# Which partitions 80 rows of each wq-gradient group are sent from, and how the last gradients are stored, in a decode backward kernel

## The chip, the core and the metric

The kernel runs on one core of a Trainium2 chip. The metric is the device time of one execution in microseconds (us), the median of several runs: 729.89 us before the change (three runs, 729.66 to 730.07). Lower is better.

## The reference, cut to what matters

One token of width D = 640 goes through a layer norm, attention of 32 heads over a cache of 8192 positions, and beside it a gated MLP of width 1728. The kernel returns the output row and all gradients for a given `grad_out`.

```
xn  = layernorm(x)
q   = (xn @ wq) in 32 heads of 128;  p = softmax(q k^T / sqrt(128));  o = p v
out = x + o @ wo + (silu(xn @ w1) * (xn @ w3)) @ w2
gradients of sum(out * grad_out): x, k_cache, v_cache, wq, wo, w1, w3, w2
```

The caches are 32 x 8192 x 128 in bf16 each, so each head's K and V are 2 MB, read once, and their gradients are 2 MB each, written once. The gradient of `wq` (640 x 4096) is the outer product of xn and dq, and that of `wo` (4096 x 640) the outer product of o and `grad_out`.

## The kernel before, in words

**Heads.** The loop over h = 0 to 31 calls `head(h)`. A head's K and V lie in two of ten 2 MB buffers `kv0` to `kv9`. TensorE transposes them (L362), ScalarE copies the transposes out of PSUM (L364), TensorE forms scores and dP (L383), VectorE does the softmax's small steps (L426 to L494), TensorE sums (L477), and VectorE writes the K and V gradients over the K and V that they came from (`outer`, L510, four pieces of 128 x 4096 a head). `store` sends such a buffer to DRAM, and `load_next` then queues the next head's load into a free buffer. Loads and stores of K and V are issued by SyncE's queue (SP, `fifo` L106 and `fifo_wide` L111) in program order, so a load that waits for its buffer holds up the store behind it.

**MLP.** Before head 2 comes `mlp()`, whose weights lie in four of the ten buffers; it is followed by its weight gradients, which GpSimd (POOL) issues.

**Groups.** Heads come in eight groups of four. A group has a `wq_g` tile (128 partitions x 5 x 512: row ci * 128 + p of `wq` lies in partition p) and a `wo_g` tile. While the next group's heads run, the group's gradients are made (`fin_od`, `fin_pe`, `fin_wo`, `fin_wq`, spread over the heads by `side_k`, `side_m` and `side_v`), and GpSimd issues their stores. `fin_wq(g, ci)` makes 128 rows of 1 KB and sends them with an indirect DMA (`scatter`, L330): `row_idx` gives each partition its row in DRAM, and a row whose index is out of bounds is left out.

**Rows that leave from elsewhere.** `rel_setup`, called once ahead of the head loop, makes two sets of indices. It pushes out of bounds the indices of partitions 16 to 19 and 48 to 51 in the first four of the five ci. Those 32 rows of a group are made a second time in the tile `rel`, whose partitions 0 to 15 and 32 to 47 hold them (each partition scales the same row `dqb` by its own xn value, `rel_x`), and one more scatter with `rel_idx` sends them at the end of the group. All other indices of `rel_idx` are out of bounds.

**The last group.** Group 7 has no scatter. `store_group` (L549 to L555) sends its `wo_g` and `wq_g` in three transfers each: partitions 0 to 67 on SP's queue, 68 to 72 and 73 to 127 on GpSimd's.

**Order.** The order on each engine is the program's; nothing is rescheduled. In the prologue VectorE, TensorE and GpSimd do `rel_setup` between `rows_act(0)` and `head(0)`:

```
    rows_act(0)
    rel_setup()
    for h in range(H):
        if h == MLP_AT:
        ...
        head(h)
        if h < 2:
            nc.gpsimd.tensor_copy(gate[:], hd[h]["rdot"][:])
            load_group(h + 1, nc.gpsimd)
```

In `head(1)` the first steps are `outers_a(0)` (VectorE: both pieces of dV and one of dK of head 0, then dV's store) and the rest of head 1's K transposes (TensorE). `mx` (L426) is the first VectorE step that the scores of the head need, `col`, `fin_od` and others belong to later heads.

Of the kernel before, what the change touches and what calls it, by code (L numbers as in the profile page):

```python
# [21 lines left out]
def kernel(  # L22
# [22 lines left out]
    nc = tc.nc  # L45
# [14 lines left out]
    consts = ctx.enter_context(tc.tile_pool(name="consts", bufs=1))  # L60
# [20 lines left out]
    dwq_v = out_4.rearrange("(ci p) n -> p ci n", p=P)  # L81
    dwo_v = out_5.rearrange("(h p) c -> p h c", p=P)
# [22 lines left out]
    def fifo(out_, in_):  # L105
        nc.sync.dma_start(out_, in_)  # L106
# [10 lines left out]
    def load_group(g, eng):  # L117
        wq_g = wpool.tile([P, NC, GW], BF16, name="wq_g", tag="wq_g")
        eng.dma_start(wq_g[:], wq_v[:, :, g * GW:(g + 1) * GW])
        wo_g = wpool.tile([P, GH, D], BF16, name="wo_g", tag="wo_g")  # L120
        eng.dma_start(wo_g[:], wo_v[:, g * GH:(g + 1) * GH, :])
        grp[g] = dict(wq=wq_g, wo=wo_g)
# [47 lines left out]
    ident_f = consts.tile([P, P], F32, name="ident_f")  # L170
# [4 lines left out]
    pm_one = masks[:, 0:2]  # L175
# [45 lines left out]
    def pst():  # L221
        return ps_t.tile([P, 512], F32, name="pT", tag="pT")
# [5 lines left out]
    for ci in range(NC):  # L228
        nc.tensor.matmul(ps_xg[:, ci:ci + 1], lhsT=x_row[:, ci * P:(ci + 1) * P], rhs=one_bf[0:1, :],
                         start=True, stop=True)  # L230
        nc.tensor.matmul(ps_xg[:, NC + ci:NC + ci + 1], lhsT=g_row[:, ci * P:(ci + 1) * P], rhs=one_bf[0:1, :],
                         start=True, stop=True)
    nc.tensor.matmul(ps_xg[:, P:P + D - 512], lhsT=one_bf[0:1, :].to_broadcast([1, P]), rhs=g_row[:, 512:D],
                     start=True, stop=True)
    nc.tensor.matmul(ps_g[:], lhsT=one_bf[0:1, :].to_broadcast([1, P]), rhs=g_row[:, 0:512],
                     start=True, stop=True)
# [59 lines left out]
    NF4 = 4  # L296
    dwq_row = out_4.rearrange("d (k n) -> (d k) n", n=GW)
    row_idx = consts.tile([P, NC], I32, name="row_idx")
    rel_idx = consts.tile([P, 1], I32, name="rel_idx")
    rel_x = consts.tile([P, 1], F32, name="rel_x")  # L300
    rel = consts.tile([P, GW], BF16, name="rel")
    NREL = 48

    def rel_setup():
        nc.gpsimd.memset(rel[:], 0.0)
        w = kt_tile()[:].rearrange("p k w -> p (k w)")
        iv, off, far = w[:, 0:NC], w[:, 8:9], w[:, 16:17]
        nc.gpsimd.iota(row_idx[:], pattern=[[NG * P, NC]], base=0, channel_multiplier=NG)
        nc.vector.tensor_copy(iv, row_idx[:])
        ps_r = pst()  # L310
        for k, src in enumerate((xn_col[:], iv)):
            sx = w[:, 128 * (k + 1):128 * (k + 1) + NREL]
            nc.vector.memset(sx, 0.0)
            for b0 in (0, 32):
                nc.vector.tensor_tensor(
                    sx[:, b0:b0 + 4 * NF4].rearrange("p (c b) -> p c b", b=4),
                    src[:, 0:NF4].unsqueeze(2).to_broadcast([P, NF4, 4]),
                    ident_f[:, 16 + b0:20 + b0].unsqueeze(1).to_broadcast([P, NF4, 4]), ALU.mult)
            nc.tensor.matmul(ps_r[0:NREL, k:k + 1], lhsT=sx, rhs=pm_one[:, 0:1], start=True, stop=True)
        nc.vector.tensor_copy(rel_x[0:NREL], ps_r[0:NREL, 0:1])  # L320
        nc.vector.memset(far, 1048576.0)
        for b0 in (0, 32):
            nc.vector.tensor_copy(far[b0:b0 + 4 * NF4], ps_r[b0:b0 + 4 * NF4, 1:2])
        nc.vector.tensor_copy(rel_idx[:], far)
        nc.vector.tensor_reduce(off, ident_f[:, 16:80].rearrange("p (s r) -> p s r", r=32)[:, :, 0:4], AX.XY, ALU.add)
        nc.vector.tensor_scalar(off, off, 1048576.0, None, ALU.mult)
        nc.vector.tensor_scalar(row_idx[:, 0:NF4], iv[:, 0:NF4], off, None, ALU.add)
# [90 lines left out]
    def rows_act(h):  # L418
        qd = small.tile([P, 2, DH], BF16, name="qd")
        nc.scalar.copy(qd[:].rearrange("p a d -> p (a d)"), hd[h].pop("ps_r"))  # L420
        hd[h]["qd"] = qd
# [124 lines left out]
        for hh in range(GH):  # L546
            out_row(G_["od_bf"][:, hh, 0:1], G_["wo"][:, hh, :])

    def store_group(g, dst, t):  # L549
        if g < NG - 1:  # L550
            nc.gpsimd.dma_start(dst, t[:])  # L551
            return
        fifo(dst[0:68], t[0:68])
        for lo, hi in ((68, 73), (73, P)):
            nc.gpsimd.dma_start(dst[lo:hi], t[lo:hi])  # L555

    def fin_wo(g):
        G_ = grp[g]
        for hh in range(GH):
            nc.vector.tensor_scalar(G_["wo"][:, hh, :], g_bc[:], G_["od"][:, hh, 0:1], None, ALU.mult)  # L560
        store_group(g, dwo_v[:, g * GH:(g + 1) * GH, :], G_["wo"])

    def fin_wq(g, ci):
        G_ = grp[g]
        wq_g, dqb = G_["wq"], G_["dqb"]
        nc.vector.scalar_tensor_tensor(wq_g[:, ci, :], wq_g[:, ci, :], 1.0, dqb, ALU.mult, ALU.mult,  # L566
                                       accum_out=dxa[:, ci, g:g + 1])
        nc.vector.tensor_scalar(wq_g[:, ci, :], dqb, xn_col[:, ci:ci + 1], None, ALU.mult)
        dwq_g = dwq_v[:, :, g * GW:(g + 1) * GW]
# [222 lines left out]
    def head(h):  # L792
        nxt = h + 1 < H
        pre = nxt and h + 1 != MLP_AT
        has_prev = h > 0 and h != MLP_AT
        had = (4 if h else 2) if h != MLP_AT else 0
        if nxt:
            new_head(h + 1)
        if has_prev:
            outers_a(h - 1)  # L800
        side_k(h)
        for c in range(had, NCH, 2):
            T(h, "K", c)
# [12 lines left out]
        mx(h)  # L816
        Mp(h, "V", 0)
        T(h, "V", 4)
        mx_bc(h)
        side_m(h)  # L820
        T(h, "V", 5)
        Mp(h, "V", 2)
        expo(h)
        T(h, "V", 6)
        zsum(h)
        probs(h)
        if has_prev:
            outers_b(h - 1)
        side_pe1(h)
        T(h, "V", 7)  # L830
        side_pe1b(h)
        Mp(h, "V", 4)
        side_pe2(h)
        side_v(h)
        if nxt:
            fill_qz(h + 1)
            rows_pe(h + 1, pst()[:, 0:2 * DH], True)
            rows_act(h + 1)
        if pre:
            T(h + 1, "K", 0)  # L840
            T(h + 1, "K", 1)
        Mp(h, "V", NCH - 2)
        ev(h, "V")
        o_sum(h)
        selm(h, "V")
        rdot(h)
        if pre:
            T(h + 1, "K", 2)
        dsum(h)
        if pre:  # L850
            T(h + 1, "K", 3)
            Mp(h + 1, "K", 0)
        dq_sum(h)
        if not nxt:
            col(h)
# [90 lines left out]
```

## Time and profile before

| what | value |
|---|---|
| median of three runs | 729.89 us |
| the profiled execution, its own time | 733.47 us |
| its span, first to last instruction | 731.7 us |
| bytes moved, mean rate | 303.53 MB, 415 GB/s |
| TensorE matmul busy | 603.5 us, 82% |
| VectorE busy | 462.5 us, 63% |
| ScalarE busy | 376.9 us, 52% |
| GpSimd busy | 83.7 us, 11% |
| scatters of `wq_g` / of `rel` | 35 / 7, median 8.7 / 7.9 us from issue to landing |

The page's part 2 cuts the span into 40 slices of 18.3 us and gives each engine's busy share in tenths, then the share of time in which the 16 DMA engines had a packet, and the rate. Part 4 follows the work that ended last back to the start. The windows view sums the same for stretches that are asked for; there a DMA packet is counted in the stretch in which it starts. Beside these the trace holds each DMA packet (start, duration, size, queue, without the number of its engine) and each rise of a semaphore; a transfer over all 16 DMA engines raises its semaphore 16 times, once for each engine.

### The profile page before, as it was taken

How to read it: one execution, taken by the hardware profiler on the slowest of the kernel's cores; microseconds unless marked ns; L12 is line 12 of the kernel's file. 1: busy time of each engine (PE TensorE's matmuls, PEld its weight loads, DVE VectorE, ACT ScalarE, POOL GpSimd, SP SyncE). 2: the span in 40 equal slices, each digit the busy share in tenths (PEclk: the TensorE clock that was granted, in tenths of full speed). 3: DMA queues.
4: the chain of work that ended last, by engine and by line, in shares of the span. 5: the costliest groups of instructions: out<-in, count | busy, mean ns of one | idle time of the engine just before them, and what ended most of it. 6: DMA issues, size and time to landing. Idle time of an engine off the chain costs nothing.

```text
span 731.7 us, 13091 instructions
## 1 busy us (share of the span) xinstructions
PE 603.5 (82%) x5213; PEld 377.1 (52%) x5213; DVE 462.5 (63%) x829; ACT 376.9 (52%) x727; POOL 83.7 (11%) x84
## 2 busy tenths in 40 slices
PE   3989579999999999978896999788979889888820
PEld 2556456665566556545554556355545555555510
DVE  4168665777867886857645775656665676646780
ACT  3650726666666656645554556355655455545500
POOL 0010010002220011101110111011200110011110
PEclk9995799999999999999998999999999899989955
DMA  9999999999999999999999999999999999999994
GB/s 355 391 417 412 437 427 389 409 414 408 419 421 419 426 425 430 413 436 425 428 421 432 426 432 422 429 425 430 435 417 423 437 428 423 429 436 425 426 425 169
DMA packets 24554, 303.53 MB, mean 415 GB/s; under 512 B 3715, under 2 KB 5691, under 8 KB 11822
## 3 DMA queue, kind: packets, MB, share of 16 engines
q1 hardware_dynamic: 17994, 277.09, 89.8%
q0 software_dynamic: 6496, 25.61, 8.8%
q8 instruction: 41, 0.67, 0.4%
q14 instruction: 19, 0.16, 0.1%
q10 hardware_dynamic: 4, 0.00, 0.0%
HBM read 151.34 MB, written 152.26 MB: 415 GB/s over the span
## 4 chain that ended last, share of the span: by engine, by line
DMA 49%; PE 37%; DVE 7%; ACT 4%; issue 1%; SPq 0%; ACTq 0%; DVEq 0%
DMA out_dram<-kv 21%; PE pT L362 17%; DMA kv<-in_A_k_cache_dram 15%; DMA kv<-in_A_v_cache_dram 11%; PE sA L383 5%; PE dA L383 4%; PE X L477 3%; DVE kv L510 3%; PE m L400 2%; DMA wo_g<-in_A_wo_dram 2%; ACT KT L364 1%; ACT kv L689 1%; PE gu_ps L608 1%; PE dh_ps L619 1%; PE acc L203 1%
## 5 line engine op out<-in xcount | busy, mean ns | idle before, releaser
L364 ACT COPY KT<-pT 128x512 f32<-128x512 f32 x512 | 288.5, 588 | 224.1 <-PE pT L362 205.2
L362 PE MATMUL pT<-ident_f,kv 128*128 128x128 f32 x2048 | 307.3, 289 | 56.3 <-DMA kv<-in_A_k_cache_dram 38.0
L362 PEld LDWEIGHTS pT<-ident_f,kv 128*128 128x128 f32 x2048 | 236.5, 148 | 147.7 <-PE pT L362 51.9
L510 DVE TENSOR_TENSOR kv<-qd,U 128x4096 bf16<-128x4096 bf16 x64 | 146.0, 2284 | 0.0
L510 DVE TENSOR_TENSOR kv<-qd,P 128x4096 bf16<-128x4096 bf16 x64 | 143.6, 2284 | 0.0
L477 PE MATMUL X<-kv,Z 128*32 128x512 bf16 x1024 | 95.3, 408 | 1.8 <-DVE Z L494 1.8
L330 POOL DMA_INDIRECT out_dram<-wq_g,row_idx x35 | 49.1, 1403 | 333.4 <-DMA out_dram<-wq_g,row_idx 137.6
L383 PE MATMUL dA<-KT,qz 128*32 128x512 bf16 x512 | 84.5, 410 | 0.0
L383 PE MATMUL sA<-KT,qz 128*32 128x512 bf16 x512 | 82.3, 401 | 0.0
L460 DVE SCALAR_TENSOR_TENSOR U<-m,P 128x64 bf16<-128x64 f32 x32 | 7.4, 232 | 95.7 <-PE m L400 95.7
L477 PEld LDWEIGHTS <-Z 128*32 128x32 bf16 x1024 | 32.6, 101 | 35.5 <-issue 8.3
L383 PEld LDWEIGHTS <-qz 128*32 128x32 bf16 x1024 | 29.6, 95 | 41.0 <-issue 38.4
L426 DVE TENSOR_REDUCE mrow<-m 128x1 f32<-128x64 f32 x32 | 7.1, 222 | 56.3 <-PE m L400 54.5
L400 PE MATMUL m<-selc,KT 64*128 64x64 f32 x256 | 30.3, 240 | 7.5 <-ACT KT L390 7.5
L400 PEld LDWEIGHTS m<-selc,KT 64*128 64x128 f32 x256 | 21.3, 142 | 28.8 <-ACT KT L390 19.9
L420 ACT CAST qd<-pT 128x256 bf16<-128x256 f32 x32 | 11.9, 372 | 40.0 <-DVE kv L510 30.4
L433 DVE TENSOR_REDUCE negM<-m 128x1 f32<-128x128 f32 x32 | 9.3, 291 | 32.8 <-PE m L430 31.8
L566 DVE SCALAR_TENSOR_TENSOR wq_g<-wq_g,side 128x512 bf16<-128x512 bf16 x40 | 27.3, 682 | 0.0
L261 DVE SCALAR_TENSOR_TENSOR side<-wo_g,g_bc 128x640 bf16<-128x640 bf16 x32 | 26.2, 820 | 0.9 <-DMA wo_g<-in_A_wo_dram 0.5
L492 DVE SCALAR_TENSOR_TENSOR U<-m,P 128x128 bf16<-128x128 f32 x32 | 11.4, 355 | 15.8 <-PE m L490 15.8
L390 ACT COPY KT<-dA 64x512 f32<-64x512 f32 x32 | 18.6, 581 | 4.2 <-PE dA L383 4.2
L551 POOL DMA_DIRECT2D out_dram<-wo_g x7 | 5.4, 768 | 124.0 <-DVE qz L407 124.0
(179 smaller groups left out, 402.4 us busy)
## 6 DMA issues: line engine op xcount, KB each, us to landing
out_dram<-kv SPq DMA_DIRECT2D x64, 2048.0 KB
kv<-in_A_k_cache_dram SPq DMA_DIRECT2D x32, 2048.0 KB
kv<-in_A_v_cache_dram SPq DMA_DIRECT2D x32, 2048.0 KB
wq_g<-in_A_wq_dram POOLq DMA_DIRECT2D x7, 640.0 KB, 15.9
wo_g<-in_A_wo_dram POOLq DMA_DIRECT2D x7, 640.0 KB, 23.3
out_dram<-wo_g POOLq DMA_DIRECT2D x7, 640.0 KB, 19.3
kv<-in_B_w_dram SPq DMA_DIRECT2D x2, 1728.0 KB
out_dram<-kv POOLq DMA_DIRECT2D x2, 1728.0 KB, 24.2
```

What stands on the lines that cost most here:

```text
L261: nc.vector.scalar_tensor_tensor(junk[:], G_["wo"][:, hh, :], 1.0, g_bc[:], ALU.mult, ALU.mult, accum_out=G_["do"][:, hh:hh + 1])
L330: nc.gpsimd.indirect_dma_start(dst, bass.IndirectOffsetOnAxis(ap=idx, axis=0), src, None, element_offset=g * GW, bounds_check=bound, oob_i ...
L362: nc.tensor.transpose(pT[:, k * P:(k + 1) * P], W3[:, 4 * c + k, :], ident_f[:])
L364: nc.scalar.copy(KT[:].rearrange("p k w -> p (k w)"), pT[:])
L383: nc.tensor.matmul(S_[kind][q:q + QW, :], lhsT=S_["qz"][:, o:o + QW], rhs=KTb[c][:, par, :], start=(c0 == 0 and par == 0), stop=(c0 == NCH ...
L390: nc.scalar.copy(XS[0:QH].rearrange("p k w -> p (k w)"), S_.pop(kind)[0:QH, :])
L400: nc.tensor.matmul(S_["m"][:, b0:b0 + 4 * J].rearrange("p (x c k t) -> p k x c t", x=4, k=4, t=2)[:, k], lhsT=XS[0:QH, k, :], rhs=selc[0:Q ...
L420: nc.scalar.copy(qd[:].rearrange("p a d -> p (a d)"), hd[h].pop("ps_r"))
L477: nc.tensor.matmul(xg["X"][q:q + QW, :], lhsT=Z[:, o:o + QW], rhs=W[:, N4 * i:N4 * (i + 1)], start=(slot == 0 and i < 4), stop=(slot == NS ...
L492: nc.vector.scalar_tensor_tensor(S_["U2"][:], S_["V"][:, 0:J].unsqueeze(2).to_broadcast([P, J, 2]), S_["m"][:, OC + NS:OC + NS + 1], S_["P ...
L510: nc.vector.tensor_tensor(dst[:, lo * DH:hi * DH].rearrange("p (j a b) -> p j a b", a=DH // 2, b=2), vec.rearrange("p (a b) -> p a b", b=2 ...
L566: nc.vector.scalar_tensor_tensor(wq_g[:, ci, :], wq_g[:, ci, :], 1.0, dqb, ALU.mult, ALU.mult, accum_out=dxa[:, ci, g:g + 1])
```

## The change

The rows that leave from elsewhere become 80 a group instead of 32, in 20 blocks of four partitions. `FROM` lists the blocks that are taken out for each ci, `TO` the partitions of `rel` that send them: ten blocks with a scatter after ci = 0, ten with a scatter after ci = 4, so there are two `rel` scatters a group. The title of the change names the partitions by DMA engines: those of 0, 2, 7, 8 and 15 send (in the order of `TO`, two blocks each), instead of those of 4, 10, 11, 13 and 12. `rel_setup` is rewritten for this: a loop over the 20 blocks, with two VectorE instructions each, and it is called at h = 1, ahead of `head(1)`, instead of ahead of `head(0)`. GpSimd's clearing of `rel` is gone, and its `iota` comes behind the loads of group 1. The last group's `wo_g` and `wq_g` go out in one plain transfer each, over all 128 partitions, on GpSimd's queue.

```
-    NREL = 48
+    TO = (0, 32, 8, 40, 28, 60, 64, 96, 92, 124)
+    FROM = ((16, 48, 72, 76), (16, 48, 104, 84), (16, 48, 108, 116), (16, 48, 72, 84), (16, 48, 76, 80))
     def rel_setup():
-        nc.gpsimd.memset(rel[:], 0.0)
...
         nc.gpsimd.iota(row_idx[:], pattern=[[NG * P, NC]], base=0, channel_multiplier=NG)
+        nc.vector.tensor_copy(ix, row_idx[:])
+        blocks = [(ci, k, b) for ci in range(NC) for k, b in enumerate(FROM[ci])]
         ps_r = pst()
...
+        for s in range(2):
+            nc.vector.memset(w[:, 0:256], 0.0)
+            for (ci, k, b), to in zip(blocks[s * len(TO):], TO):
+                nc.vector.tensor_scalar(w[:, to:to + 4], ident_f[:, b:b + 4], xn_col[:, ci:ci + 1], None, ALU.mult)
+                nc.vector.scalar_tensor_tensor(w[:, P + to:P + to + 4], ident_f[:, b:b + 4], ix[:, ci:ci + 1],
+                                               ident_f[:, b:b + 4], ALU.mult, ALU.mult, accum_out=moved[:, ci, k:k + 1])
+            for k in range(2):
+                nc.tensor.matmul(ps_r[:, 2 * k + s:2 * k + s + 1], lhsT=w[:, P * k:P * (k + 1)], rhs=pm_one[:, 0:1],
+                                 start=True, stop=True)
+        nc.vector.tensor_copy(rel_x[:], ps_r[:, 0:2])
+        for s in range(2):
+            at = ps_r[:, 2 + s:3 + s]
+            nc.vector.tensor_scalar(gone, at, -8192.0, FAR, ALU.mult, ALU.add)
+            nc.vector.tensor_scalar(gone, gone, 0.0, at, ALU.max, ALU.add)
+            nc.vector.tensor_copy(rel_idx[:, s:s + 1], gone)
+        nc.vector.tensor_reduce(off, moved, AX.X, ALU.add)
+        nc.vector.tensor_scalar(off, off, 8192.0, FAR, ALU.mult, ALU.min)
+        nc.vector.tensor_tensor(off, off, ix, ALU.add)
+        nc.vector.tensor_copy(row_idx[:], off)
...
-    def store_group(g, dst, t):
-        if g < NG - 1:
-            nc.gpsimd.dma_start(dst, t[:])
-            return
-        fifo(dst[0:68], t[0:68])
-        for lo, hi in ((68, 73), (73, P)):
-            nc.gpsimd.dma_start(dst[lo:hi], t[lo:hi])
...
     def fin_wo(g):
-        store_group(g, dwo_v[:, g * GH:(g + 1) * GH, :], G_["wo"])
+        nc.gpsimd.dma_start(dwo_v[:, g * GH:(g + 1) * GH, :], G_["wo"][:])
...
     def fin_wq(g, ci):
-            if ci == NC - 1:
-                nc.vector.tensor_scalar(rel[0:NREL], dqb[0:NREL], rel_x[0:NREL], None, ALU.mult)
-                scatter(dwq_row, (D - 1) * NG, rel[:], rel_idx[:], g)
+            if ci in (0, NC - 1):
+                s = min(ci, 1)
+                nc.vector.tensor_scalar(rel[:], dqb, rel_x[:, s:s + 1], None, ALU.mult)
+                scatter(dwq_row, (D - 1) * NG, rel[:], rel_idx[:, s:s + 1], g)
...
-                store_group(g, dwq_g, wq_g)
+                nc.gpsimd.dma_start(dwq_v[:, :, g * GW:(g + 1) * GW], wq_g[:])
...
     rows_act(0)
-    rel_setup()
     for h in range(H):
+        if h == 1:
+            rel_setup()
         if h == MLP_AT:
```

More of the change, by code (lines that the diff above doesn't have):

```diff
@@ L295 @@
     I32 = mybir.dt.int32
-    NF4 = 4
+    FAR = 1048576.0
     dwq_row = out_4.rearrange("d (k n) -> (d k) n", n=GW)
     row_idx = consts.tile([P, NC], I32, name="row_idx")
-    rel_idx = consts.tile([P, 1], I32, name="rel_idx")
-    rel_x = consts.tile([P, 1], F32, name="rel_x")
+    rel_idx = consts.tile([P, 2], I32, name="rel_idx")
+    rel_x = consts.tile([P, 2], F32, name="rel_x")
     rel = consts.tile([P, GW], BF16, name="rel")
-    NREL = 48
+    TO = (0, 32, 8, 40, 28, 60, 64, 96, 92, 124)
@@ L304, in rel_setup @@
+    FROM = ((16, 48, 72, 76), (16, 48, 104, 84), (16, 48, 108, 116), (16, 48, 72, 84), (16, 48, 76, 80))
+    assert NC == len(FROM) and 2 * len(TO) == sum(map(len, FROM))
     def rel_setup():
-        nc.gpsimd.memset(rel[:], 0.0)
         w = kt_tile()[:].rearrange("p k w -> p (k w)")
-        iv, off, far = w[:, 0:NC], w[:, 8:9], w[:, 16:17]
+        ix = w[:, 256:256 + NC]
+        moved = w[:, 264:264 + 4 * NC].rearrange("p (c b) -> p c b", b=4)
+        off, gone = w[:, 288:288 + NC], w[:, 296:297]
@@ L308, in rel_setup @@
         nc.gpsimd.iota(row_idx[:], pattern=[[NG * P, NC]], base=0, channel_multiplier=NG)
-        nc.vector.tensor_copy(iv, row_idx[:])
+        nc.vector.tensor_copy(ix, row_idx[:])
+        blocks = [(ci, k, b) for ci in range(NC) for k, b in enumerate(FROM[ci])]
         ps_r = pst()
[L311 to L327, printed above, removed]
+        for s in range(2):
[7 more added lines that the diff above has]
+                                 start=True, stop=True)
@@ L568, in fin_wq @@
         nc.vector.tensor_scalar(wq_g[:, ci, :], dqb, xn_col[:, ci:ci + 1], None, ALU.mult)
-        dwq_g = dwq_v[:, :, g * GW:(g + 1) * GW]
         if g < NG - 1:
             scatter(dwq_row, (D - 1) * NG, wq_g[:, ci, :], row_idx[:, ci:ci + 1], g)
-            if ci == NC - 1:
-                nc.vector.tensor_scalar(rel[0:NREL], dqb[0:NREL], rel_x[0:NREL], None, ALU.mult)
-                scatter(dwq_row, (D - 1) * NG, rel[:], rel_idx[:], g)
+            if ci in (0, NC - 1):
+                s = min(ci, 1)
+                nc.vector.tensor_scalar(rel[:], dqb, rel_x[:, s:s + 1], None, ALU.mult)
+                scatter(dwq_row, (D - 1) * NG, rel[:], rel_idx[:, s:s + 1], g)
         if ci == NC - 1:
             if g == NG - 1:
-                store_group(g, dwq_g, wq_g)
+                nc.gpsimd.dma_start(dwq_v[:, :, g * GW:(g + 1) * GW], wq_g[:])
             grp.pop(g)
```

## The prediction

> **What bounds the kernel now.** First the page's part 2, for the DMA engines:
>
> ```profile
> DMA  9999999999999999999999999999999999999994
> GB/s 355 391 417 412 437 427 389 409 414 408 419 421 419 426 425 430 413 436 425 428 421 432 426 432 422 429 425 430 435 417 423 437 428 423 429 436 425 426 425 169
> ```
>
> They are busy in every slice but the last. Then the windows view, cut where I looked for gaps. Columns: stretch, length, busy time of the five engines, clock, DMA share, GB/s.
>
> ```profile
> 123.00:127.00 4.00, 4.00 (x31) 2.22 (x30) 4.00 (x3) 2.93 (x6) 0.00 (x0) 1.00 0.70 285
> 127.00:400.00 273.00, 246.89 (x2179) 153.78 (x2178) 191.47 (x323) 161.03 (x325) 36.37 (x29) 0.98 1.01 421
> 400.00:715.00 315.00, 257.57 (x2164) 158.02 (x2164) 200.53 (x338) 158.13 (x312) 37.98 (x34) 0.91 1.01 428
> 715.00:720.00 5.00, 0.00 (x0) 0.00 (x0) 0.00 (x0) 0.00 (x0) 0.00 (x0) 0.50 0.78 291
> 720.00:725.00 5.00, 0.00 (x0) 0.00 (x0) 0.00 (x0) 0.00 (x0) 0.00 (x0) 0.50 0.45 157
> 725.00:730.00 5.00, 0.00 (x0) 0.00 (x0) 0.00 (x0) 0.00 (x0) 0.00 (x0) 0.50 0.13 42
> ```
>
> From 127 to 715 us nobody idles (1.01: packets overlap by 4 ns). Time is lost in two places. At the end the share falls to 0.78, 0.45, 0.13: some engines are done while others still work. And at 123 to 127 us it is 0.70: the engines ran dry, because the store that comes next waits for VectorE:
>
> ```profile
> 125.29 0.34 SPq L106 DMA_DIRECT2D out_dram<-kv  x1
> ```
>
> Up to there the chain of waits is TensorE, VectorE and ScalarE without a pause from 17 us on. So **before 125 us computing sets the time, after 127 us DMA bytes do**: a microsecond of computing lost before 125 us is a microsecond of idle DMA, and nothing later gives it back. The change touches both places.
>
> **The end: levelled engines.** The trace's 16 semaphore rises of the store issued at 682.43 us (one for each DMA engine) come 0, 0.1, 1.3, 1.7, 1.8 | 5.2, 5.7, 5.8, 5.9, 5.9, 6.2 | 7.7, 7.9, 8.5, 8.5, 9.0 us after the first, at 698.42. At 132 us all 16 came within 0.7. So the engines drift apart: five are ahead, mean 5.1. Behind that store each engine has 24 packets of 16 KB at 0.607 us (from start to start), 14.6 us, so its K and V are done at 713.0 + its lag.
>
> The old tail adds 5 rows of `wo_g` and `wq_g` (10 KB each) on most engines and 17 on the four that the 68-row transfers use; on those, 68 packets of 1280 B (52 ns from start to start) and 85 of 1024 B (42) make 7.1 us. They end last: the rises of their `wq_g` transfer are at 726.38, 726.58, 727.83 and 730.10 us, the last of the run 730.28. The plain transfers give each engine 8 rows: 8 packets of 5120 B (0.196) and 10 of 4096 B (0.155), 3.1 us.
>
> Moved rows: four rows of 1 KB go in one 4096 B packet, 39 ns a row. Left-out rows show as 16 B packets of 11 ns: nothing. The order of `TO` and `FROM` and the engines in the title tell how partitions belong to engines: four neighbours, and those 32 further on. For seven groups, after less before: engines 7, 8, 15 send 16 more rows a group, +4.4 us; 0 and 2, 16 instead of 8, +2.2; 1 and 3 lose 8, -2.2; 4 loses 8 more, -2.2; 10, 11, 13 lose 12, -3.3; 12 loses 4, -1.1; 5, 6, 9, 14 stay. Engine 4 can be found in the trace (it alone has 16 B packets in the first four scatters): its lag is 5.2, so it falls to 3.0. Of the four engines of the 68-row transfers two end their `wo_g` share at 719.4 and 720.2, the others at 724.2 and 726.5: two are of the five ahead, as 0 and 2 should be. The other numbers no row shows. If the five ahead are 0, 2, 7, 8, 15, they rise from 0 to 1.8 to 3.5 to 6.2; 5, 6, 9, 14 stay at about 6; 10, 11, 13 come to 4.4 to 5.7; 12 is between 7.7 and 9.0 now, then 6.6 to 7.9. The last engine's lag is 6.2 to 7.9; I take 7.0, the lower half, since 12 is as likely any of the slow. End: 713.0 + 7.0 + 3.1 + 0.5 (the slowest rises of the last dK, 723.78 and 725.19, are -0.1 and +1.3 against the same sum of before, 713.0 + 9.0 + 2.0) = 723.6 against 730.28: -6.7; bounds -5.2 and -7.5. With the small last output transfers, **-6.5 us**.
>
> The second `rel` scatter costs the engines nothing of note. On GpSimd it adds some 9 us a group (the scatters come every 9 us, each behind the landing of the last); the last one of group 6 goes from 688.85 to about 698, lands by 705, and the next GpSimd transfer is at 705.11. The cover is gone if it lands later. VectorE gets one more step of 0.34 us a group; it waits for loads then.
>
> **The start: `rel_setup`.** Removed from the prologue: it is on the chain there.
>
> ```profile
> 17.69 0.03 DVE qz L407
> ...
> 18.43 0.58 PE pT L319 x4
> 19.00 1.90 PE pT L362 x8
> ```
>
> TensorE's matmuls before it (L414) end at 18.08, so L362 could start at about 18.05: **-0.9 us** (0.5 to 1.2, as the clock rises only later).
>
> Added at h = 1. Each engine's new order: on VectorE behind L494 of head 0 and ahead of `outers_a(0)`; on TensorE behind the sums of head 0 and ahead of head 1's transposes; on GpSimd the `iota` behind two loads:
>
> ```profile
> 37.72 1.06 POOL L119 DMA_DIRECT2D wq_g<-in_A_wq_dram  x1
> 38.77 0.81 POOL L121 DMA_DIRECT2D wo_g<-in_A_wo_dram  x1
> ```
>
> So (in times of before) the `iota` ends at 39.75, and VectorE, which could go on at 38.51, starts at 39.8. Prices from rows with a scalar from memory on a few elements:
>
> ```profile
> 10.27 0.23 DVE L244 SCALAR_TENSOR_TENSOR xn_col<-x_col,negmean 128x5 f32<-128x5 f32 x1
> 10.42 0.08 DVE L244 DVE_READ_ACCUMULATOR xn_col<-x_col,negmean 128x1 f32 x1
> ...
> 20.03 0.23 DVE L327 TENSOR_SCALAR row_idx<-KT 128x4 int32<-128x4 f32 x1
> ```
>
> Independent VectorE steps follow each other 0.08 us before the last one's end (L646 to L648: 0.166 long, 0.083 apart), so 0.15 + 0.15 a block; where an unrelated step follows a READ_ACCUMULATOR (L407 behind L261) both start together, so that one is free. Ten blocks 2.95, the clearing of 256 columns 0.3 (L696: 320 columns, 0.325): 3.3 us, done at 43.2. TensorE, free since 39.9, waits, then two matmuls of 0.3 (L319: four in 0.58); VectorE waits for these (same tile), makes the second ten, 47.0; matmuls to 47.4. The eleven small steps behind, mostly dependent, at 0.19 to 0.27 (L649 to L651, L326, L327): 1.9 us. `outers_a(0)` starts at 49.4 instead of 38.51, 10.9 us late. Next in line:
>
> ```profile
> 38.51 4.49 DVE L510 TENSOR_TENSOR kv<-qd,P 128x4096 bf16<-128x4096 bf16 x2
> ...
> 46.13 0.22 DVE L426 TENSOR_REDUCE mrow<-m 128x1 f32<-128x64 f32 x1 [0.94 <-PE m L400]
> ```
>
> VectorE had 0.94 us of waiting there, and some 0.8 in the steps to L450, where TensorE's own work was the longer; TensorE itself is 7.5 late and no longer last. 10.9 - 1.7 = 9.1 us, less 0.9: **+8.2 us**. From L450 on the chain of head 1 and of the MLP has no slack, so the store at 125.29 comes at 133.5, and the DMA engines idle 8.2 us longer. Bounds: +3 (each step 0.08, accumulators free) and +11 (accumulators at 0.08 each, dependent steps dearer). I take 8.2, by the rows that match the shapes.
>
> **Sum.** +8.2 - 6.5 = +1.7 us: 733.47 becomes 735.2 in a profiled run. The median was 3.58 below that run; with the same distance 729.89 + 1.7 = **731.6 us**.
>
> **Rivals.**
> - The setup is cheaper or hidden: DMA work is queued till the store comes, or the small steps run at 0.08. Against it is the share of 0.70 before the change: there is no spare work, and the step durations. At +3 the sum is -3.5, 726.4; fully hidden 722.5.
> - The receivers aren't ahead: if 7, 8 and 15 lie in the middle now (lag 6), they get to 10.4, the end to 727.0 (713.0 + 10.4 + 3.1 + 0.5), the gain is 3.3, and with the setup 729.89 + 4.9 = 734.8. For it: no row numbers them. Against: five engines are ahead, two of them rightly placed. The Trainium skill, page "DMA: Bandwidth & Descriptors", section "Latency and other measured facts", speaks for this rival: it has engines 7 and 15 as usually slower than the others in traces, with a cause marked as a guess. By that rule the change loads the wrong engines. The trace has five engines early, not two late, so I give it little.
> - The change doesn't move what it says (left-out rows still cost a packet): the 16 B packets of today's left-out rows speak against it, and I leave it at next to nothing.
> - The setup is dearer: +11, sum +4.5, 734.4.
>
> **Chances.** The forecast, setup exposed and engines levelled, net 0 to +3.5: 0.60; cheaper setup 0.20; wrong receivers 0.13; dearer setup 0.07. What a measurement of this kernel tells from no change is about 0.2%, 1.46 us. Of the forecast two thirds lie over it (0.39) and a third within (0.21); of the cheap setup 0.13 is faster, 0.07 within; the last two are slower. Slower 0.59, same 0.28, faster 0.13. The range that leaves 0.2 out: 727.6 to 734.8.
>
> **What would show it.** In the trace after: L362 of head 0 starts near 18.0 instead of 19.0; TensorE sits idle twice around 39 to 47 us behind the new matmuls; the first dV store goes out near 53 instead of 43.02; the DMA share has a gap of about 9 us somewhere between 120 and 135; the rises of the last stores lie within some 4 us instead of 9; the DMA share drops from 1 to 0 in 3 to 5 us at the end instead of 15. A gap that isn't wider than before would make the forecast wrong by 8 us, a spread that stays at 9 by 3 to 6.

## The result, and the profile after

The changed kernel takes **734.32 us** (median of seven runs, 732.91 to 736.96), the kernel before 730.07 in the same session: a ratio of 1.0061, 95% interval 1.0042 to 1.0080. So it is 4.3 us slower, where +1.7 was forecast. The profiled execution of the changed kernel took 733.57 us, near its median. That of the kernel before took 733.47, which is 3.4 above its median; a second profile of it, below, is the better one to compare with.

The page's part 2 of the changed kernel, DMA share and rate in 40 slices:

```profile
DMA  9999999899999999999999999999999999999997
GB/s 353 396 414 368 429 434 385 343 399 435 416 429 415 436 421 420 429 431 417 426 431 432 414 435 428 431 417 426 431 423 431 429 419 431 430 431 425 427 392 314
```

The eighth slice (128 to 146 us) is now an 8 with 343 GB/s, and the last is fuller (7 and 314 instead of 4 and 169). The fourth (55 to 73 us) falls from 412 to 368 GB/s, though its share is still a 9. The windows view of the changed kernel (stretch, length, busy time of TensorE, weight loads, VectorE, ScalarE, GpSimd, clock, DMA share, GB/s):

```profile
65.00:70.00 5.00, 5.00 (x88) 4.97 (x88) 5.00 (x3) 0.00 (x0) 0.00 (x0) 0.50 0.92 255
...
124.00:140.00 16.00, 15.41 (x134) 9.66 (x132) 13.32 (x21) 9.55 (x21) 0.00 (x0) 1.00 0.75 296
...
705.00:710.00 5.00, 3.79 (x46) 1.52 (x42) 4.29 (x7) 1.10 (x3) 0.53 (x1) 1.00 0.82 342
710.00:715.00 5.00, 1.06 (x8) 0.97 (x8) 5.00 (x3) 0.66 (x2) 1.75 (x1) 0.79 0.93 379
...
720.00:725.00 5.00, 0.00 (x0) 0.00 (x0) 4.82 (x16) 0.00 (x0) 0.80 (x1) 0.50 0.99 395
725.00:732.00 7.00, 0.93 (x3) 0.58 (x3) 2.16 (x12) 0.00 (x0) 0.90 (x1) 0.50 0.43 153
```

Behind the MLP the share is 0.75, a wider gap, as forecast. There is a second hole ahead of it that the share hardly shows: at 65 to 70 us the engines are 0.92 busy and move 255 GB/s, where they moved 413 and 418 in the two profiles of the kernel before. At the end the share is near 1 up to 725 us, but there are holes at 705 to 715, and TensorE and VectorE still work in them: computing is late there, which the prediction did not have. The waits view says the same:

```profile
DVE rel L571 <- DMA out_dram<-rel,rel_idx: 65.9, 5, 13.5
```

VectorE waited 65.9 us, in five groups, up to 13.5 us at a time, before it could write `rel` for the second set: the first set's scatter still read the same tile. GpSimd's timeline at the end (start, duration, line, transfer, idle time before and its releaser):

```profile
709.47 2.28 POOL L336 DMA_INDIRECT out_dram<-wq_g,row_idx  x1 [7.20 <-DVE Z L500]
717.55 0.97 POOL L336 DMA_INDIRECT out_dram<-rel,rel_idx  x1 [5.80 <-DVE kv L516]
720.35 0.80 POOL L559 DMA_DIRECT2D out_dram<-wo_g  x1 [1.82 <-DVE wo_g L558]
725.63 0.90 POOL L575 DMA_DIRECT2D out_dram<-wq_g  x1 [4.48 <-DVE dxn L891]
```

The last `rel` scatter is issued at 717.55 and lands at 725.1. The one of the kernel before was issued at 688.85. Each scatter waits for the landing of the one before it, 7 to 11 us; the first of a group, which is queued behind the loads of a new group and a `wo_g` store, takes 24. Seven of them make 85.5 us a group.

### The profile page after: what moved, and what is told of

It reads as the page before. It is cut to its first block, busy times and chain, and to the rows that moved or that the text cites. A ratio compares the mean times of both kernels' runs of the same rounds, so it can differ in the third digit from the quotient of the medians.

```text
span 731.8 us, 13164 instructions
## 1 busy us (share of the span) xinstructions
PE 595.6 (81%) x5210; PEld 372.9 (51%) x5217; DVE 472.4 (65%) x895; ACT 372.5 (51%) x727; POOL 93.8 (13%) x88
## 4 chain that ended last, share of the span: by engine, by line
PE 52%; DMA 23%; DVE 14%; ACT 6%; issue 3%; POOL 0%; SPq 0%; ACTq 0%; POOLq 0%; DVEq 0%
PE pT L368 24%; DMA out_dram<-wq_g,row_idx 17%; DVE kv L516 8%; PE sA L389 7%; DMA out_dram<-rel,rel_idx 5%; PE dA L389 5%; PE X L483 4%; ACT KT L370 3%; PE m L406 3%; DMA wo_g<-in_A_wo_dram 2%; ACT kv L687 1%; PE gu_ps L606 1%; ACT KT L396 1%; PE pT L270 1%; PE acc L203 1%
## 5 line engine op out<-in xcount | busy, mean ns | idle before, releaser
L368 PE MATMUL pT<-ident_f,kv 128*128 128x128 f32 x2048 | 301.9, 285 | 0.0
L368 PEld LDWEIGHTS pT<-ident_f,kv 128*128 128x128 f32 x2048 | 231.9, 147 | 87.7 <-PE pT L368 54.8
L483 PE MATMUL X<-kv,Z 128*32 128x512 bf16 x1024 | 93.5, 412 | 56.5 <-DVE Z L459 55.1
L389 PE MATMUL sA<-KT,qz 128*32 128x512 bf16 x512 | 83.8, 408 | 0.0
L389 PE MATMUL dA<-KT,qz 128*32 128x512 bf16 x512 | 80.9, 394 | 0.0
L571 DVE TENSOR_SCALAR rel<-side,rel_x 128x512 bf16<-128x512 bf16 x14 | 4.9, 349 | 65.9 <-DMA out_dram<-rel,rel_idx 65.9
L336 POOL DMA_INDIRECT out_dram<-rel,rel_idx x14 | 20.5, 1462 | 194.6 <-DMA out_dram<-wq_g,row_idx 119.6
```

The costliest lines, as they stand in the source:

```text
L336: nc.gpsimd.indirect_dma_start(dst, bass.IndirectOffsetOnAxis(ap=idx, axis=0), src, None, element_offset=g * GW, bounds_check=bound, oob_i ...
L368: nc.tensor.transpose(pT[:, k * P:(k + 1) * P], W3[:, 4 * c + k, :], ident_f[:])
L389: nc.tensor.matmul(S_[kind][q:q + QW, :], lhsT=S_["qz"][:, o:o + QW], rhs=KTb[c][:, par, :], start=(c0 == 0 and par == 0), stop=(c0 == NCH ...
L483: nc.tensor.matmul(xg["X"][q:q + QW, :], lhsT=Z[:, o:o + QW], rhs=W[:, N4 * i:N4 * (i + 1)], start=(slot == 0 and i < 4), stop=(slot == NS ...
```

## The experiments

Three theories: **S**, the setup at h = 1 idles the DMA engines (the prediction's main term). **A**, the added `rel` scatter (its tile, then its chain) makes the end late. **L**, the moved rows and plain last transfers don't gain what was forecast. Ratios are to the kernel before of the same session (medians 730.07 to 730.74), with 95% intervals; "idle" is the mean idle time of a DMA engine, "busy" the mean time in which it has a packet, both summed from the trace's packets (to some 0.2 us, as packets overlap a little).

### One `rel` step less; the setup ahead of head 4

```
-                nc.vector.tensor_scalar(rel[:], dqb, rel_x[:, s:s + 1], None, ALU.mult)
+                if s == 0:
+                    nc.vector.tensor_scalar(rel[:], dqb, rel_x[:, s:s + 1], None, ALU.mult)
```

> The changed kernel, except that the `rel` rows of the second scatter of a group are not scaled again (VectorE's step for s = 1 is left out, so those 40 rows of a group carry the factors of the first set); the scatters, rows, queues and the setup stay. It takes away VectorE's wait for the landing of the first `rel` scatter (65.9 us in five groups, up to 13.5 each) and 7 x 0.35 us of work. Theory A (this wait makes computing the last thing to end): the wait group is gone, TensorE waits for K and V loads again (in the kernel before 38.0 + 18.1 us, in the changed one none), the last dK store is issued near 702 to 706 instead of 717.5, the 1.3 us of idle DMA at 706 to 714 and the 1.9 us at 726 to 730 go: 3.2 us off the changed kernel, 731.1 us against its median of 734.3. Rival B (the setup at h = 1 alone makes the loss): no change, 734.3. Rival C (the moved rows and the plain last transfers cost by themselves): the stores come earlier, but the time stays within 1 us of 734.3, with engines ending over 10 us apart.

Measured: 735.88 us, 1.0064 (1.0045 to 1.0083). Theory A's expectations failed: the wait did not go, it moved (63.5 us, at the step of the next group's first set, which now waits for the last scatter).

```
-        if h == 1:
+        if h == 4:
             rel_setup()
```

> The changed kernel with `rel_setup` called ahead of head 4 instead of head 1. Theory A: the store that follows the MLP goes out near 124.5 instead of 130.50 and the DMA engines lose 0 to 1 us there instead of 4.2; but the setup's 10 us are still on the chain of computing, which by the waits for `rel` is what ends last, so the last dK store stays within 2 us of 717.5 and the time within 1 us of 734.3. Rival B (the gap at 126 to 131 us makes the loss): 3.6 us less, 730.7.

Measured: 736.03 us, 1.0072 (1.0051 to 1.0093). No gain, as A said; but not for A's reason alone, and the last dK store goes out at 720.2, a little outside A's 2 us. The DMA idle time did not go, it moved: 0.04 us at 110 to 140 and 6.1 us behind 140, where head 4 runs. There too each load goes out right behind the store that frees its buffer (stores at 130.80 and 150.19 us, loads at 131.37 and 150.63), so the engines live on the next store.

### The wait alone, the tail alone

```
-            if ci == NC - 1:
+            if ci in (0, NC - 1):
                 nc.vector.tensor_scalar(rel[0:NREL], dqb[0:NREL], rel_x[0:NREL], None, ALU.mult)
                 scatter(dwq_row, (D - 1) * NG, rel[:], rel_idx[:], g)
```

> The kernel before with the making of `rel` and its scatter done twice a group (after ci = 0 and after ci = 4, the same 32 rows both times): the second scatter and the wait alone, no other rows moved, the old setup, the old last transfers. Theory A: VectorE waits some 50 to 70 us for `rel` in five groups, TensorE's 56 us of waiting for loads fall to under 10, the last dK store is issued at 708 to 712 instead of 702.3. As the old tail ends with the slowest engines, which have work queued until then, and those ahead run dry, the time rises by 0 to 3 us: 730 to 733. What the prediction took for granted (the second step waits when VectorE waits for loads anyway): VectorE's new wait stands, but stores and time don't move by more than 0.3 us.

Measured: 733.83 us, 1.0044 (1.0022 to 1.0065): 3.1 us more than before. VectorE waits 64.2 us for `rel`, and the last dK store goes out at 713.1 (702.3 before). Both the store and the time lie about 1 us over what A gave. So what the prediction costed at nothing costs 3 us where nothing else is late.

```
...
-        store_group(g, dwo_v[:, g * GH:(g + 1) * GH, :], G_["wo"])
+        nc.gpsimd.dma_start(dwo_v[:, g * GH:(g + 1) * GH, :], G_["wo"][:])
...
-                store_group(g, dwq_g, wq_g)
+                nc.gpsimd.dma_start(dwq_v[:, :, g * GW:(g + 1) * GW], wq_g[:])
```

> The kernel before with only the plain last transfers (the last group's wo_g and wq_g in one transfer each over 128 partitions on GpSimd's queue); rows and setup as before. By the sums of the prediction the slowest engine (9.0 us behind) ends at 713.0 + 9.0 + 3.1 + 0.5 = 725.6 instead of 730.28: 4.7 us less, 725.4. Rival: the 68-row transfers lay on engines that are ahead, so they levelled the end already, and spreading them alike lets the slowest ones end later: 0 to 3 us more, 730 to 733.

Measured: **726.38 us**, 0.9939 (0.9921 to 0.9956), 4.4 us less than before. The plain transfers alone give most of what the prediction hoped for from the whole end, and this kernel beats both.

### Neither tie: `rel` made once; and the rows alone

```
-                nc.vector.tensor_scalar(rel[:], dqb, rel_x[:, s:s + 1], None, ALU.mult)
+                if g == 0 and s == 0:
+                    nc.vector.tensor_scalar(rel[:], dqb, rel_x[:, s:s + 1], None, ALU.mult)
```

> Taking away one of the two `rel` steps a group changed nothing: the wait went to the other step. So theory A is put more sharply. The seven scatters of a group go one behind the other on GpSimd, 85.5 us a group in the changed kernel, and as each `rel` step waits for the landing of the scatter before, VectorE, and with it all computing, goes at that pace from the second group on (85.2 to 85.6 us a group; where nothing holds computing up it takes 70.4). Here `rel` is made once, in group 0 (left out: its scaling in the other groups, so the moved rows of groups 1 to 6 carry group 0's values); all scatters, moved rows, the setup at h = 1 and the plain last transfers stay. Theory A: VectorE's wait for `rel` is gone; computing runs at 70.4 us for a second group, then waits for loads as in the kernel before (TensorE 30 us or more); last dK store at 702 to 706; the scatters still go one behind the other and the last lands near 715 to 720, so the last wo_g and wq_g wait for them on GpSimd's queue. Time 726 to 731, some 5.5 us under the changed kernel's 734.3. Rival B (the setup's 10 us and the added steps eat the lead): last dK store at 714 or later, time within 1 us of 734.3.

Measured: 735.15 us, 1.0055 (1.0037 to 1.0073). Computing is back at the pace of before (a second group at 70.4 us, last dK store at 706.3, TensorE waits for loads again), and the time did not move. Theory A as "VectorE is tied" has fallen for the changed kernel. GpSimd's timeline of this run:

```profile
720.23 0.97 POOL L336 DMA_INDIRECT out_dram<-rel,rel_idx  x1 [6.99 <-DMA out_dram<-wq_g,row_idx]
721.20 0.80 POOL L559 DMA_DIRECT2D out_dram<-wo_g  x1
727.09 0.89 POOL L576 DMA_DIRECT2D out_dram<-wq_g  x1 [5.08 <-DMA out_dram<-rel,rel_idx]
```

The scatters still go one by one, and the last `wq_g` store waits for the landing of the last (726.5). But the last dK store lands only at 728.1 in this run, so the engines' own bytes are as late as the chain.

```
...
-        nc.gpsimd.dma_start(dwo_v[:, g * GH:(g + 1) * GH, :], G_["wo"][:])
+        (nc.gpsimd if g < NG - 1 else nc.sync).dma_start(dwo_v[:, g * GH:(g + 1) * GH, :], G_["wo"][:])
...
-                nc.gpsimd.dma_start(dwq_v[:, :, g * GW:(g + 1) * GW], wq_g[:])
+                nc.sync.dma_start(dwq_v[:, :, g * GW:(g + 1) * GW], wq_g[:])
...
```

> The kernel with `rel` made once, and besides the last wo_g and wq_g on SP's queue, behind no scatter, and the setup ahead of head 4: the 80 moved rows alone, with neither the tie nor the gap behind the MLP (left out: the scaling of `rel` in groups 1 to 6). It is to be compared with the kernel before with plain last transfers, 726.4 us, which moves 32 rows. Theory that the receivers are the engines that are ahead: the rises of the last K/V stores lie within 6 us instead of 9, and the time is 2 to 3 us less than 726.4: 723.9. Rival (the receivers lie in the middle, or 7 and 15 late): the rises lie 9 us apart or more, the time is 726.4 or above.

Measured: 735.32 us, 1.0066 (1.0043 to 1.0090). As a test of the rows alone it failed: the setup ahead of head 4 idles the engines 4.9 us, and the last `wq_g` store, on SP's queue too, waits for the last scatter (727.24). The rises lie within 6 us, as expected.

### 40 rows; no rows

```
-    FROM = ((16, 48, 72, 76), (16, 48, 104, 84), (16, 48, 108, 116), (16, 48, 72, 84), (16, 48, 76, 80))
+    FROM = ((16, 48, 72), (16, 48, 76), (16, 48, 84), (80,), ())
...
-        for s in range(2):
+        for s in range(1):
...
-            if ci in (0, NC - 1):
-                s = min(ci, 1)
+            if ci == NC - 1:
+                s = 0
...
-        if h == 1:
+        if h == 4:
```

> The changed kernel with one set of ten blocks instead of two (partitions 16 and 48 for ci 0 to 2, 72, 76, 84 and 80 once each: 40 rows a group), so one `rel` step and one scatter of `rel`, at the end of the group, six scatters a group; setup ahead of head 4; plain last transfers. A whole kernel, nothing left out. Theory A: six scatters take some 62 to 76 us a group, so the tie is gone: VectorE waits less than 5 us for `rel`, computing gets its second group at 70.4 us, the last dK store is near 702. The slowest engines lose 4 rows a group, 1.1 us; the prologue is 0.9 us shorter. 726.4 - 1.1 - 0.3 = 725.0 (724 to 726.5). Rival B (any `rel` rows from five engines, or the setup wherever it stands, cost): 730 or more.

Measured: 729.17 us, 0.9985 (0.9967 to 1.0003). Between the two expectations: the tie is gone, but half a setup ahead of head 4 still idles the engines 2.1 us.

```
...
-                nc.vector.tensor_scalar(rel[0:NREL], dqb[0:NREL], rel_x[0:NREL], None, ALU.mult)
-                scatter(dwq_row, (D - 1) * NG, rel[:], rel_idx[:], g)
...
```

> The kernel before with plain last transfers and no rows moved at all: no setup beyond the iota, no `rel`, five scatters a group. What is a moved row worth? Theory of the prediction (a row is 39 ns of its engine): engine 4 gets back 32 rows a group in seven groups, 8.7 us, and comes from 5.2 us behind the first to 13.9, 4.9 us later than the slowest of today: 726.4 + 4.9 = 731.3, with two or fewer engines over 11 us behind. Rival (rows cost nothing as long as others work): 725.5 to 726.5.

Measured: 732.80 us, 1.0028 (1.0012 to 1.0044), 6.4 us above the kernel with the tail alone. The rises of the dV or dK store issued at 685.4 come 0, 0.4, 0.5, 0.5, 0.8 | 4.7, 4.9, 7.1 to 10.4 | 17.9 us after the first: one engine alone is late. So moving rows does move time, 32 rows a group some 12.7 us of one engine (17.9 against the 5.2 of engine 4 in the prediction; over 224 rows 57 ns each, where it had 39).

### The chain alone, the setup alone

```
-            if ci in (0, NC - 1):
-                s = min(ci, 1)
+            if ci == NC - 1:
+                s = 1
```

> With `rel` made once (no tie to VectorE), the time stayed at 735: computing was back at the pace of before, but the seven scatters of a group still went one behind the other until 727 us, and the last wq_g store waits for the landing of the last of them. So theory A in its third form: the chain of scatters alone (85 us a group with seven, from 170 us on) sets the end, and the setup at h = 1 costs on top. Here the changed kernel loses its first `rel` step and scatter of a group and nothing else (left out: the 40 rows a group of the first set are written by nobody), so there are six scatters a group; setup at h = 1, plain last transfers. Theory A: the last scatter is issued near 690 to 695, the last wq_g store near 711 to 716; the time is that of the kernel before with plain last transfers, 726.4, plus the setup's gap (5 us more idle DMA at 110 to 140 us), less about 1 us for engines that are better levelled: 730.4 (729 to 732), 4 us under the changed kernel. Rival (the setup at h = 1 and the moved rows make the whole loss): within 1 us of the changed kernel, 733.5 to 735.5.

Measured: 733.85 us, 1.0036 (1.0023 to 1.0050). The chain is short (last scatter at 696.36), VectorE waits for no `rel`, and yet the time is the rival's. By the ratios the changed kernel lies 1.8 us above it, give or take 1.7, and 40 rows a group less to write (0.29 MB, 0.7 us at 415 GB/s) are part of that. **Theory A explains 1 us or so of the loss, not 4.**

> The kernel before with plain last transfers, and the new setup of 20 blocks done besides the old one at h = 1, into tiles that nobody uses: the price of the setup by itself. The prediction's step gives 9.1 us of delay at that place (the 0.9 us of the prologue stays here) and as much DMA idle: 726.4 + 9.1 = 735.5. The trace of the changed kernel shows the delay shrink from 8.7 us in head 1 to 5.2 at the store behind the MLP (with 1 us of prologue saved): idle DMA 5 us more than without, 726.4 + 5 = 731.4 (730 to 732.5). Rival: idle engines early are made up later: 726 to 728.

Its edit: the new `rel_setup`, with index tiles of its own, added ahead of head 1 of the kernel with plain last transfers. Measured: **735.64 us**, 1.0066 (1.0044 to 1.0087), **9.3 us** above that kernel, give or take 2.0 by the two ratios. The prediction's 9.1 us is met, and my reading of the trace after (5 us) is not. Windows of the kernel with the tail alone, then of this one:

```profile
65.00:70.00 5.00, 5.00 (x28) 2.76 (x26) 3.85 (x8) 0.00 (x0) 0.00 (x0) 0.64 1.00 418
...
110.00:140.00 30.00, 29.29 (x269) 17.84 (x267) 18.94 (x36) 19.24 (x39) 0.00 (x0) 1.00 1.00 408
...
715.00:732.00 17.00, 0.00 (x0) 0.00 (x0) 0.00 (x0) 0.00 (x0) 0.00 (x0) 0.65 0.21 89
```

```profile
65.00:70.00 5.00, 5.00 (x89) 4.50 (x80) 5.00 (x3) 0.00 (x0) 0.74 (x1) 0.64 0.97 301
...
110.00:140.00 30.00, 29.70 (x250) 18.92 (x248) 14.53 (x29) 20.47 (x41) 0.20 (x1) 0.99 0.88 356
...
715.00:732.00 17.00, 0.93 (x3) 0.59 (x3) 2.48 (x14) 0.00 (x0) 0.90 (x1) 0.50 0.69 291
```

At 110 to 140 us the share falls from 1.00 to 0.88, and the work that was not done there stands at the end: 0.69 of the last 17 us instead of 0.21. The two profiled executions are 7.55 us apart (734.10 and 726.55). The store behind the MLP is 7.8 us later (131.59 and 123.81); idle time before 140 us is up by 5.0, behind 690 down by 1.0, and busy time is up by 3.5 (719.4 and 715.9): the same bytes in packets that take longer, a little in every size (16 KB 619 and 617 ns, 32 KB 1232 and 1230, 4 KB 169 and 163). About half of this lies at 60 to 100 us (4 KB packets take 249 ns at 60 to 80 us, instead of 164), in the same hole as in the changed kernel: 0.97 busy at 65 to 70 us, and 301 GB/s instead of 418. Why packets take longer there is not shown. Counted in bytes the loss is one: with the setup 3.0 MB less have been moved by 140 us, 7.1 us at the 421 GB/s of 127 to 400 us, and 3.6 MB less by 690 us.

### Setup in the shade; before once more

```
-        if h == 1:
-            rel_setup()
...
     rows_act(0)
+    rel_part1()
...
+            if h == 0 and c == 4:
+                rel_part2()
```

> A whole kernel. One set of ten blocks (the 40 rows of the run with setup ahead of head 4, which took 729.2 with 2.1 us of idle DMA between 140 and 690 us), plain last transfers, six scatters a group; the setup is cut in two and put where VectorE waits anyway: its blocks behind the prologue's last step, where VectorE waits 9.3 us for the first scores, its two matmuls and small steps inside head 0, behind the third pair of K transposes; it works in `rel` and U2_1, which are free then. Theory A: no gap behind the MLP, prologue 0.9 us shorter as TensorE has no matmul there; engines levelled as in that run (spread of the last K/V rises 8 instead of 12): 729.2 - 2.1 - 0.5 = 726.6, and up to 1.5 less by the scatter of the rate from run to run: 725 to 727. Rival (40 moved rows from five engines cost by themselves): 728 or more.

Measured: 727.73 us, 0.9952 (0.9933 to 0.9970). VectorE's timeline of this run:

```profile
20.54 0.08 DVE L321 DVE_READ_ACCUMULATOR rel<-ident_f,U 128x1 f32 x1
23.73 0.16 DVE L331 COPY rel_x<-pT 128x1 f32<-128x1 f32 x1 [3.11 <-PE pT L329]
...
24.93 0.17 DVE L340 CAST row_idx<-U 128x5 int32<-128x5 f32 x1
28.22 0.23 DVE L439 TENSOR_REDUCE mrow<-m 128x1 f32<-128x64 f32 x1 [3.12 <-PE m L413]
```

Blocks, 3.11 us of waiting, small steps, and 3.12 us of waiting still ahead of `mrow`: the setup is free here, and there is no gap behind the MLP (idle 0.2 us at 110 to 140). The time lies between the two expectations (725 to 727, 728 or more). It is below that of the kernel before and of the changed one, but not below that of the kernel with the tail alone (726.38, 0.9939; the intervals overlap): 40 rows spread over five senders gain nothing that shows.

> The kernel before, for a second profile of it: the first one belongs to an execution of 733.47 us, 3 us over the median. If the engines' packets were slower in that one (mean busy time of an engine 718.7 us, against 715.9 in the kernel with plain last transfers), this one shows 715 to 717 us of busy time, the same idle times (some 1 us at 110 to 140, 9.5 to 11 behind 690), and an execution of 729 to 731.5 us. If it was the end that was longer, the busy time is the same and the idle time behind 690 is 7 to 8 us.

Measured: 729.04 us. Windows of this second profile of the kernel before:

```profile
110.00:140.00 30.00, 29.29 (x269) 17.83 (x268) 19.23 (x36) 18.95 (x39) 0.00 (x0) 1.00 0.99 406
...
715.00:732.00 17.00, 0.00 (x0) 0.00 (x0) 0.00 (x0) 0.00 (x0) 0.00 (x0) 0.58 0.28 102
```

Against the first (0.97 and 0.40) it is both: busy time 716.9 instead of 718.7 us, idle time behind 690 us 8.5 instead of 10.6, and the gap behind the MLP hardly there (0.35 us instead of 0.97; the store comes at 123.52, not 125.29).

## Why the prediction was right or wrong

The direction held, the time lies within the range, and the setup's term was right; the size was 2.6 us short. With +4.3 it lies above the 0 to +3.5 that the chance of 0.60 was given for, and close to the times of two rivals, 734.4 (setup dearer) and 734.8 (wrong receivers). The runs show neither of these, so that the range, which reached to 734.8, held is partly luck. The terms by the runs:

| term | forecast | measured | from |
|---|---|---|---|
| setup at h = 1, less the prologue | +9.1 - 0.9 | +9.3, give or take 2.0, - 1.1 | setup alone; the prologue by the trace (from the start of L414 to that of head 0's L362 0.17 us instead of 1.23) |
| plain last transfers | within -6.5 | -4.4, give or take 1.3 | tail alone |
| moved rows | within -6.5 | -0.5, not told from 0 | what is left, if the terms add (the rises say 0.6) |
| second `rel` scatter | 0 | +1, give or take 1.7 | changed kernel less the one without it |
| sum | +1.7 | +4.3 | the changed kernel |

So 1.6 of the 2.6 us lie in the end and 1.0 in the second scatter; by the intervals, either could be the scatter of the runs.

**Step 1, what bounds it: right.** A microsecond lost before 125 us was not given back: with the setup alone, 7.8 us of delay at the store behind the MLP made 7.6 us between the profiles and 9.3 between the medians. It holds for longer than I wrote: at head 4, near 150 us, the DMA share is 1.01 in the kernel before, and the setup there still cost as much. A full share does not say that work is queued.

**The start: right up to VectorE's reciprocal.** The changed kernel's VectorE timeline:

```profile
46.95 0.16 DVE L324 COPY rel_x<-pT 128x2 f32<-128x2 f32 x1 [0.97 <-PE pT L322]
...
48.85 4.48 DVE L516 TENSOR_TENSOR kv<-qd,P 128x4096 bf16<-128x4096 bf16 x2
...
55.45 0.22 DVE L432 TENSOR_REDUCE mrow<-m 128x1 f32<-128x64 f32 x1
...
57.89 0.17 DVE L456 RECIPROCAL rZ<-m 128x1 f32<-128x1 f32 x1 [1.51 <-PE m L450]
```

`outers_a(0)` starts at 48.85 (49.4 less the 0.9 of the prologue was forecast), `mrow` has no wait left in front of it, and the reciprocal is 8.7 us later than before (8.2 forecast). The first dV store goes out at 53.36 (53), head 0's L368 (L362 before) goes on at 17.5 (18.0). Behind it the account is rougher than its sum. The store behind the MLP goes out at 130.50, not at 133.5: 5.2 us later than in the first profile of before (125.29) and 7.0 later than in the second (123.52). The gap was to be 8.2 us wider; idle time at 40 to 140 us is 4.6 us instead of 1.0 or 0.35. Besides, the packets are slower, as in the run with the setup alone: busy time 719.7 us, against 716.9 in the second profile of before. In bytes, by 140 us the changed kernel is 2.5 MB behind that profile, 6.0 us at 421 GB/s, a third of it since the hole at 65 to 70 us.

**The end, levelled engines: this is where the sum was furthest off, as far as the runs can tell.** The forecast took the last lag from 9.0 to 7.0 and got -6.5 with the short tail. (Its bound -5.2 does not come out of its terms: 713.0 + 7.9 + 3.1 + 0.5 = 724.5 is -5.8.) By the same numbers without moved rows (713.0 + 9.0 + 3.1 + 0.5 = 725.6 against 730.28) the tail alone makes -4.7, and -4.4 was measured. So the moved rows were to bring the other 1.8 us, and there the runs show less. The spread of the rises of a store issued near 675 us did fall, from 9.0 and 9.9 (the two profiles of before) to 5.2. But where nothing else is late the last engine ends the run, and it hardly came nearer to the mean of the 16: 3.4 to 4.4 us behind it in five runs that move 32 rows (one of them twice a group; 3.9 on average), 2.2 to 4.4 in six with the blocks of 80 rows taken out (3.3; the changed kernel 3.7). The five that were ahead were brought back by several us, the last was brought forward by 0.6, which is less than these kernels differ among themselves. I had only guessed which engine is last ("12 is as likely any of the slow"). The sign "the rises of the last stores lie within some 4 us" did come true (2.4 to 3.3 us for the last three K and V stores), but not by levelling: the store issued just ahead of them (698.11) still has 5.7, and then the stores wait for late computing, so that the engines ahead run dry (share 0.82 at 705 to 710 us) and the others catch up.

The rival "the receivers aren't ahead" is out. It had an engine 10.4 us behind the first; in the six kernels with the blocks of 80 rows taken out, the rises of a store issued near 675 us lie within 3.9 to 6.4 us. And with no rows moved five engines lie within 0.8 us and 4 us ahead of the others, and giving rows to 0, 2, 7, 8 and 15 closes that gap (in the 40-row kernels, which give 7, 8 and 15 eight rows a group more than before, to 1.0 and 1.6 us, from 3.3 with the tail alone). What the Trainium skill says in "DMA: Bandwidth & Descriptors", section "Latency and other measured facts", that engines 7 and 15 are usually slower, is not what these traces show, as far as the names of the title go.

**The second scatter: wrong as reasoned, nearly right in its price.** "VectorE gets one more step of 0.34 us a group; it waits for loads then" overlooked that the step writes a tile that a queued scatter still reads. "The last one of group 6 lands by 705" was 20 us off (725.1): I added 9 us to the last group, but a chain of seven, the first of 24 us, takes 85.5 us already in the second group, where computing took 70.5 before, and the 20 us lost there and in the third group (79.9 before) are never made up. Alone on the kernel before it costs 3.1 us. In the changed kernel it hides behind the setup: chain and DMA bytes both end near 727 us, and the later of two ends counts, not their sum. This fits the run with the short chain, where the time fell by 1.8 us, give or take 1.7. It is not shown from the other side: `rel` made once left the chain as long as it was, the setup at head 4 left its idle time, and no run has seven scatters without the setup's gap and with plain last transfers.

**The base.** The sum was made against an execution 3.4 us over the median, with a gap and an end that the second profile doesn't have. It went in as a constant and came out as one, so it did no harm to the forecast; read trace against trace, though, the change seems to cost nothing (733.57 and 733.47).

## What to carry to other kernels

A moved step is priced where it stands: a setup of this kind cost 9 us at head 1 (20 blocks), and nothing (10 blocks) where VectorE waits for the first scores. Where a step writes a tile that a transfer reads, count the transfer's whole queue, not its own time. And to shorten an end set by the slowest of many engines, first find out which one is last: levelling the fast ones narrowed the spread here and, as far as the runs can tell, left the time.

## What the runs showed of the hardware

- A plain transfer over all 128 partitions beat a hand-made split of it by 4.4 us. The Trainium skill ("DMA: Bandwidth & Descriptors", section "Rules for kernel authors") advises one 128-partition transfer over two on disjoint partition halves. Here the parts were 68, 5 and 55 partitions, not halves; the run agrees with the advice, and by the rises the reason here is the 68-row part, which gave four engines 17 rows each, so that they ended last (726.38 to 730.10 us).
- DMA engines drift apart over a run of 730 us: without moved rows five are some 7 to 10 us ahead of eight others, and one, with the same number of rows, is 17.9 us behind the first.
- The mean busy time of an engine for nearly the same bytes was 715.0 to 717.1 us in kernels without a tie and with a gap of 2 us at most, and 718.8 to 720.6 in those with a tie or a wider gap (718.7 in the first profile of before). That is up to 5 us, more than most edits here. In kernels with the setup at h = 1 some 1 to 2 us of it lie at 60 to 100 us; the cause of the rest is open.
- A share near 1 can hide a loss: with the setup at h = 1 the engines were 0.92 busy at 65 to 70 us and moved 255 GB/s, where the kernel before moved 418 at 1.00.
